# Second dense layer of batches 1 to 3 by one level of Strassen's method

## The chip, the cores and the metric

The kernel runs on one core of one Trainium2 chip. The metric is the device time of one execution in microseconds (us), given as the median of several executions. "Span" is the time from the first to the last instruction of the one profiled execution. It is about 2 us shorter than the time. Ratios are those of one kernel's fast runs to the other kernel's fast runs in the same rounds on the same chip. They are not quite the ratio of the medians quoted beside them.

## The reference

Four batches of attention with a window of 128 keys and 4 sink keys, then two dense layers with a squared ReLU between them:

```python
keep = is_sink | in_window                       # 8 heads, 768 tokens, head_dim 64
a = softmax(where(keep, q @ k.T / 8, -1e9)); attn = a @ v
x = attn.transpose(0, 2, 1, 3).reshape(3072, 512)
r = maximum(x @ w_in, 0)                         # w_in 512 x 2048
out = (r * r) @ w_out                            # w_out 2048 x 512
```

The change works on the last line. The result is compared with a tolerance, so sums of bf16 operands may be rounded in another order.

## The kernel before

Every piece of work is an `Op` with a key, a cost per engine, the ops it comes after and the buffers that it takes. The kernel's own plan puts the ops in order, by earliest start and then by key, and the instructions are issued in that order. The waits in the finished program are derived from what the instructions read and write.

The second dense layer treats a pair of token tiles at a time. Its accumulator is one tile in PSUM of 2 x 512 fp32 a partition. Each 512 of them are called a bank in this text. It is filled by 32 matmuls of 512 columns (only the last pair of all has two tiles, left out here):

```python
def layer2(b, u, keys, by_part=False):
    ...
    for n, (i, part) in enumerate(order):
        def mm(e, i=i, t=t, part=part, n=n):
            if n == 0:
                bank_t["y", b, u] = bank(bs, "py", [128, 2, DM], FP32)
            ...
            for fb in range(4 * part, 4 * part + 4):
                nc.tensor.matmul(pm[:, i, :], lhsT=gT_sb[t // 4][:, fb, 128 * (t % 4):128 * (t % 4) + 128],
                                 rhs=w_out_sb[:, fb, :], start=(fb == 0), stop=(fb == NFB - 1))
    ...
    def evac(e):                                 # the only reader of py
        o = bank_t["osb", b, u] = work["osb"].tile([128, 2, DM], FP32, name="osb", tag="osb")
        copy(e, o, bank_t["y", b, u])
```

The softmax here doesn't subtract the row's maximum and nothing guards it: scores larger than these inputs give would overflow.

Of the kernel before, what the change touches and what calls it, by code (L numbers as in the profile page):

```python
# [20 lines left out]
WARM_UNTIL = 34.0  # L21

# [10 lines left out]
class Op:  # L33
    def __init__(self, key, engines, run, after, takes, reads, dma, follow):
        self.key, self.engines, self.run = key, engines, run
        self.after, self.takes, self.reads, self.dma = list(after), list(takes), list(reads), dma
        self.follow, self.yields, self.margin = list(follow), [], 0.0
        self.end = self.issued = self.engine = None


class Plan:
# [8 lines left out]
    def __init__(self, capacity):  # L50
        self.ops, self.capacity = [], dict(capacity)

    def op(self, key, engines, run, after=(), takes=(), reads=(), dma=0.0, follow=()):
        o = Op(key, engines, run, after, takes, reads, dma, follow)
        self.ops.append(o)
        return o

    def run(self):
# [12 lines left out]
        while left:  # L71
            best = None
            for o in ready:
                t = 0.0
                need = {}
                for s in o.takes:
                    if len(s.pools) > 1:
                        s.pool = min(s.pools, key=lambda p: min(free[p], default=1e9))
                    need[s.pool] = need.get(s.pool, 0) + 1
                ok = True  # L80
                for p, n in need.items():
                    if len(free[p]) < n:
                        ok = False
                        break
                    t = max(t, sorted(free[p])[n - 1] + LATENCY)
                if not ok:
                    continue
                if o.dma:
                    past = landed.get(next(iter(o.engines)), ())
                    if len(past) >= 8:  # L90
                        t = max(t, past[-8])
                pick = None
                for e, c in o.engines.items():
                    slack = PE_SLACK if e == "pe" else 0.0
                    start = max([t + slack if t > 0 else 0.0, engine.get(e, 0.0)] +
                                [a.end + LATENCY + slack for a in o.after if a.engine != e or a.dma] +
                                [a.issued for a in o.follow])
                    if pick is None or start + c < pick[1] + pick[2]:
                        pick = (e, start, c)
                cand = (round(pick[1], 2), o.key)  # L100
                if best is None or cand < best[0]:
                    best = (cand, o, pick)
# [31 lines left out]
def kernel(  # L134
# [28 lines left out]
    sizes = dict(att=2, den=2, qr=5, qs=6, expm=8, r=3, osb=2)  # L163
# [9 lines left out]
    mask = consts.tile([128, 2, 4, 128], BF16)  # L173
    mask0 = consts.tile([128, 2, 4, 128], BF16)
    bias = consts.tile([128, 4, 128], BF16)
    bias0 = consts.tile([128, 4, 128], BF16)
# [10 lines left out]
    xT_sb = [consts.tile([128, NS, NKB, 256], BF16, name=f"xT{i}") for i in range(2)]  # L187
    gT_sb = [consts.tile([128, NFB, w], BF16, name=f"gT{i}") for i, w in enumerate((512, 256))]
# [63 lines left out]
    def build_masks(e):  # L252
        for h2 in range(2):
            for i in range(2):
                nc.gpsimd.tensor_copy(out=mask[:, h2, 2 * i:2 * i + 2, :], in_=tri)
                nc.gpsimd.tensor_copy(out=mask0[:, h2, 2 * i:2 * i + 2, :], in_=tri)
            nc.gpsimd.memset(mask0[0:NSINK, h2, 1:3, :], 1.0)
# [10 lines left out]
    c_fill = op(-9, {"dve": 2.5}, fill)  # L268
# [11 lines left out]
    def dma_op(queue, name, run, us, behind=None, takes=(), yields=()):  # L280

        def go(e):
            ds = run(e)
            if behind is not None:
                for d in ds:
                    after_dma(d, loaded[behind])
            loaded[name] = ds[-1]
        o = op(-5, {queue: (0.85 if queue == "pool" else 0.5) + (0.3 if behind else 0.0)}, go, dma=us, takes=takes,
               follow=[chained[queue]] if queue in chained else (),
               after=[ops[behind]] if behind is not None else ())  # L290
        ops[name] = chained[queue] = o
        o.yields += [ops[y] for y in yields]
        o.follow += [ops[y] for y in yields]
        return o

# [106 lines left out]
    def attention(b, key):  # L402
# [16 lines left out]
        def stage(g, f0, f1, side):  # L419

# [83 lines left out]
            if g == 0:  # L504
# [7 lines left out]
                def sink_values(e):  # L512
                    for j in range(NP):
# [9 lines left out]
                                    after=([ops["turn", b, 1, 0]] if b in NATURAL else copies) + prev_sinks)  # L523
            lo = max(256, t0)
# [20 lines left out]
            for s in range(t0 // 256, last // 256):  # L545
                fs = 0.36 + 0.5 * (256 * s - t0) / (last - t0)
                norms = []
                biased = b == 0 and s < BIASED
                for m0 in (0, 2):
# [27 lines left out]
                    for ms in ((m0,), (m0 + 1,)) if b == 0 else ((m0, m0 + 1),):  # L577
                        sc.append(op(
                            at(fm), {"pe": len(ms) * (0.7 if biased else 0.28) + 0.1}, lambda e, f=scores, ms=ms: f(e, ms),
                            takes=[banks[m - m0] for m in ms],  # L580
                            after=[ops["turn", b, ti, t] for ti in (0, 1)
# [5 lines left out]
                    for j, m in enumerate((m0, m0 + 1)):  # L587
# [7 lines left out]
                        def domask(e, s=s, m=m, o=o):  # L595
                            x = ex_t[b, s, m]
                            if e == "dve":
                                mk = (mask if s else mask0).rearrange("p h a c -> p h (a c)")
                                nc.vector.tensor_mul(x[:, :, o:512], x[:, :, o:512], mk[:, :, o:512])  # L599
                            elif s == 0:  # L600
                                mk = mask0.rearrange("p h a c -> p h (a c)")
                                nc.gpsimd.tensor_mul(x[:, :, o:512], x[:, :, o:512], mk[:, :, o:512])
# [4 lines left out]
                        if biased:  # L607
# [4 lines left out]
                                         {"pool": 1.3, "dve": 0.7} if s else {"dve": 0.58, "pool": 1.1},  # L612
                                         domask, after=[ex] if first else [ex, late["masks"]]))

                    bo = Slot(side, 1)

# [35 lines left out]
                    norms.append(op(at(fm + 0.17), {"dve": 0.95}, norm, after=[va] + prev_bridge, reads=[bo]))  # L652

# [30 lines left out]
    def layer1(b, key, fbs, c0, cw, need):  # L684
        n = len(fbs)
# [14 lines left out]
        def relu(e):  # L700
            r = bank_t[tag, "r"] = work["r"].tile([128, n, cw], BF16, name="r", tag="r")
            if e == "act":
                nc.scalar.activation(out=r, in_=bank_t.pop(tag), func=AF.Relu)  # L703
            else:
                nc.vector.tensor_scalar_max(r, bank_t.pop(tag), 0.0)
# [9 lines left out]
    def layer2(b, u, keys, by_part=False):  # L715

        tail = b == B - 1 and u == NS - 1
        bs = Slot("den", 1)
        bt_ = Slot("den", 1)
# [4 lines left out]
        for n, (i, part) in enumerate(order):  # L724
            t = 2 * u + i

            def mm(e, i=i, t=t, part=part, n=n):
                if n == 0:
                    bank_t["y", b, u] = bank(bs, "py", [128, 2, DM], FP32)
                if tail and n == 4:  # L730
                    bank_t["y", b, u, 1] = bank(bt_, "py", [128, 2, DM], FP32)
                pm = bank_t["y", b, u, 1] if tail and n >= 4 else bank_t["y", b, u]
                for fb in range(4 * part, 4 * part + 4):
# [5 lines left out]
                   takes=[bs] if n == 0 else [bt_] if tail and n == 4 else ())  # L739
# [9 lines left out]
        def store(e):  # L749
            nc.sync.dma_start(out=out[128 * g:128 * g + 256, :].rearrange("(i p) m -> p i m", p=128),  # L750
                              in_=bank_t.pop(("osb", b, u)))

        def evac_tail(i):
            def run(e):
                if i == 0:
                    bank_t["osb", b, u] = work["osb"].tile([128, 2, DM], FP32, name="osb", tag="osb")
                o, y = bank_t["osb", b, u], bank_t["y", b, u] if i == 0 else bank_t["y", b, u, 1]
                if i == 0:
                    copy("dve", o[:, 0, :], y[:, 0, :])
                    nc.sync.dma_start(out=out[128 * g:128 * g + 128, :], in_=o[:, 0, :])  # L760
                else:
                    h = work["qr"].tile([128, DM // 2], FP32, name="half", tag="qr")
                    copy("act", h, y[:, 1, 256:512])
                    copy("dve", o[:, 1, 0:256], y[:, 1, 0:256])
                    nc.scalar.dma_start(out=out[128 * g + 128:128 * g + 256, 256:512], in_=h)
                    nc.sync.dma_start(out=out[128 * g + 128:128 * g + 256, 0:256], in_=o[:, 1, 0:256])
            return run

        if tail:
            e0 = op(keys(0, 3), {"dve": 0.7}, evac_tail(0), after=[ops["layer2", b, 2 * u, 3]], takes=[os_], reads=[bs])  # L770
            op(keys(1, 3), {"dve": 0.5}, evac_tail(1), after=[a, e0], reads=[bt_, os_])
        else:
            ev = op(keys(1, 3), {"act": 1.05, "dve": 1.25}, evac, after=[a], takes=[os_], reads=[bs])
            op(keys(1, 3), {"sp": 0.1}, store, after=[ev], reads=[os_], dma=2.0)
# [32 lines left out]
    for b in range(B):  # L807
        if b == 0:
            at = attention(0, lambda f: f - 1.0)
            at(0, 0.0, 1.0, ("den", "att"))  # L810
            late["masks"] = op(0.006, {"pool": 3.0}, build_masks, after=[c_tri, ops["bridge", 0, 1]])
# [23 lines left out]
        for u in range(NS):  # L835
            if b == 0 and u < 2:
                layer2(b, u, lambda i, part, u=u: 0.408 + 0.466 * (4 * part + 2 * u + i) / 24, by_part=True)
            else:
                layer2(b, u, lambda i, part, u=u, b=b: b + 0.5 + 0.5 * (8 * u + 4 * i + part) / 24)
# [36 lines left out]
```

## Time and profile before

| | before |
|---|---|
| time, median of 3 | 225.88 us (225.76 to 226.05) |
| span of the profiled run | 223.8 us |
| TensorE busy | 215.5 us, 96% |
| VectorE busy | 103.7 us, 46% |
| all waits of TensorE, summed | 3.1 us, of which 0.6 after the first 20 us |
| last matmul to end of span | 3.9 us |

TensorE is the bound: busy in every slice and hardly ever waiting. The prediction shows the lines. The waits tell whether the order of the other engines keeps TensorE fed, and the last row is what no saving on TensorE can touch.

### The profile page before, as it was taken

To read this page: it belongs to the slowest core of one execution; us is meant where nothing else is said; L and a number is where in the kernel's file an instruction comes from. 1 tells how busy PE (TensorE), PEld (TensorE's weight loads), DVE (VectorE), ACT (ScalarE), POOL (GpSimd) and SP (SyncE) were. 2 spreads that over 40 slices of the span, in tenths; PEclk is the share of its full clock that TensorE was granted. 3 is DMA by queue.
4 is the path that set the end of the run, shared out by engine and by line. 5 is a ranking of instruction groups with operands and counts; after the bars stand their busy time and mean duration, and the time that the engine had idled before them with its cause. 6 is when DMAs were issued, how large, how long until landed. Compare 5 with 4: busy or idle time off the path is not lost.

```text
span 223.8 us, 4586 instructions
## 1 busy us (share of the span) xinstructions
PE 215.5 (96%) x1932; PEld 138.2 (62%) x1952; DVE 103.7 (46%) x192; ACT 115.9 (52%) x131; POOL 64.8 (29%) x99
## 2 busy tenths in 40 slices
PE   7899999999999999999999999999999999999993
PEld 7549996467865886555454545598464455874441
DVE  6646346476656764466452536657241024430010
ACT  2695566506893577286727188665351165551010
POOL 7991015055999415997100000000000000000000
PEclk9999999999999999999999999999999999999999
DMA  5999968998999999999999464020221320000222
GB/s 144 289 187 208 208 196 109 199 349 240 131 179 139 150 197 150 122 150 199 143 144 124 139 166 48 0 50 0 47 98 25 116 97 0 0 3 0 94 103 86
DMA packets 84309, 28.13 MB, mean 126 GB/s; under 512 B 70336, under 2 KB 80832, under 8 KB 84288
## 3 DMA queue, kind: packets, MB, share of 16 engines
q0 software_dynamic: 52608, 10.49, 61.9%
q1 hardware_dynamic: 31496, 17.20, 34.9%
q8 instruction: 15, 0.25, 0.4%
q10 hardware_dynamic: 184, 0.14, 0.2%
q14 instruction: 6, 0.05, 0.1%
HBM read 27.30 MB, written 6.29 MB: 150 GB/s over the span
## 4 chain that ended last, share of the span: by engine, by line
PE 91%; DMA 3%; SPq 2%; ACT 1%; DVE 1%; issue 1%; DVEq 0%
PE pm L694 38%; PE py L734 37%; PE po L634 6%; PE ps L571 5%; DMA qr<-in_q_dram 3%; PE pt L476 2%; SPq L348 2%; PE px L671 1%; DVE qkT L208 1%; PE ps L564 1%; PE pk L531 0%; ACT r L703 0%; ACT expm L590 0%; ACT qkT L206 0%; PE px L201 0%
## 5 line engine op out<-in xcount | busy, mean ns | idle before, releaser
L734 PE MATMUL py<-w_out_sb,gT 128*128 128x512 bf16 x366 | 86.1, 379 | 1.1 <-issue 0.3
L694 PE MATMUL pm<-xT,w_in_sb 128*128 128x256 bf16 (+1 forms) x576 | 86.7, 308 | 0.4 <-ACT r L703 0.3
L694 PEld LDWEIGHTS <-w_in_sb 128*128 128x128 bf16 x576 | 63.0, 114 | 20.9 <-issue 1.7
L703 ACT ACTIVATE r<-pm 128x1024 bf16<-128x1024 f32 x48 | 49.2, 1025 | 32.7 <-PE pm L694 23.9
L734 PEld LDWEIGHTS <-gT 128*128 128x128 bf16 x384 | 35.4, 98 | 39.2 <-issue 1.7
L710 DVE TENSOR_TENSOR gT<-r 128x1024 bf16<-128x1024 bf16 x48 | 33.1, 690 | 50.3 <-ACT r L703 50.2
L590 ACT ACTIVATE expm<-ps 128x1024 bf16<-128x1024 f32 (+1 forms) x48 | 43.2, 952 | 17.1 <-PE ps L571 17.1
L599 DVE TENSOR_TENSOR expm<-expm,mask 128x1024 bf16<-128x1024 bf16 (+1 forms) x39 | 25.4, 654 | 23.7 <-ACT expm L590 23.2
L206 ACT ACTIVATE osb<-py 128x1024 f32<-128x1024 f32 x9 | 9.2, 1024 | 31.2 <-PE py L734 31.1
L634 PEld LDWEIGHTS <-expm 128*128 128x128 bf16 x352 | 16.5, 97 | 4.1 <-issue 0.6
L634 PE MATMUL po<-v,expm 128*128 128x65 bf16 x352 | 17.5, 193 | 0.0
L646 DVE TENSOR_TENSOR xn_sb<-po,rc 128x512 bf16<-128x512 f32 x24 | 16.6, 691 | 0.8
L571 PE MATMUL ps<-qkT 64*128 64x128 bf16 (+1 forms) x256 | 14.8, 238 | 0.3
L571 PEld LDWEIGHTS <-qkT 64*128 64x128 bf16 x256 | 8.0, 94 | 10.7 <-issue 9.9
L634 PE MATMUL po<-vs,es 128*128 128x65 bf16 x128 | 13.1, 193 | 0.0
L208 DVE COPY osb<-py 128x1024 f32<-128x1024 f32 (+2 forms) x4 | 3.6, 889 | 19.0 <-PE py L734 15.9
L210 POOL CAST qs<-qr 128x512 bf16<-128x512 f32 x6 | 4.2, 714 | 26.2 <-DVE gT L710 14.1
L634 PEld LDWEIGHTS <-es 128*128 128x128 bf16 x128 | 11.7, 97 | 0.0
L390 POOL DMA_DIRECT2D v<-in_v_dram x12 | 10.8, 918 | 3.4 <-DMA qn<-in_q_dram 2.5
L380 POOL DMA_DIRECT2D qn<-in_q_dram x12 | 10.8, 918 | 1.5 <-DMA qn<-in_k_dram 1.2
L361 POOL DMA_DIRECT2D v<-in_v_dram x12 | 10.9, 926 | 0.5 <-DMA qr<-in_k_dram 0.5
L208 DVE CAST qs<-qr 128x512 bf16<-128x512 f32 x16 | 8.1, 513 | 6.2 <-DMA qr<-in_k_dram 3.1
(51 smaller groups left out, 108.1 us busy)
## 6 DMA issues: line engine op xcount, KB each, us to landing
out_dram<-osb SPq DMA_DIRECT2D x11, 512.0 KB, 2.8
v<-in_v_dram POOLq DMA_DIRECT2D x24, 128.0 KB, 6.5
qr<-in_k_dram SPq DMA_DIRECT2D x8, 256.0 KB, 5.2
qr<-in_q_dram SPq DMA_DIRECT2D x8, 256.0 KB, 4.9
w_in_sb<-in_moe_w_in_dram POOLq DMA_DIRECT2D x4, 512.0 KB, 9.8
w_out_sb<-in_moe_w_out_dram POOLq DMA_DIRECT2D x4, 512.0 KB, 10.8
qn<-in_k_dram POOLq DMA_DIRECT2D x12, 128.0 KB, 7.2
qn<-in_q_dram POOLq DMA_DIRECT2D x12, 128.0 KB, 8.8
```

What stands on the lines that cost most here:

```text
L208: nc.vector.tensor_copy(out=dst, in_=src)
L361: return [nc.gpsimd.dma_start(out=v_sb[b % 2][:, t, :, 0:D], in_=v[b, :, 128 * t:128 * t + 128, :].rearrange("h p d -> p h d"))]
L380: return [nc.gpsimd.dma_start(out=qn_t[b, ti][:, t, :].rearrange("p (h d) -> p h d", d=D), in_=(q, k)[ti][b, :, 128 * t:128 * t + 128, :]. ...
L571: nc.tensor.matmul(ps[:, h2, o:o + w], lhsT=qkT_sb[r, m, 1, c, :], rhs=qkT_sb[r, m, 0, qb:qb + w // 128, :], start=(i == 0 and not biased) ...
L590: nc.scalar.activation(out=x[:, :, o:512], in_=bank_t["s", b, s, m][:, :, o:512], func=AF.Exp, scale=scale)
L599: nc.vector.tensor_mul(x[:, :, o:512], x[:, :, o:512], mk[:, :, o:512])
L634: nc.tensor.matmul(pv[:, i, h2, :], lhsT=lhsT, rhs=rhs, start=(n_ == 0), stop=(n_ == len(mms) - 1))
L646: nc.vector.tensor_tensor(out=xn_sb[:, 2 * s:2 * s + 2, 128 * m0:128 * m0 + 256].rearrange("p i (j h d) -> p j i h d", j=2, d=D), in0=pv[: ...
L694: nc.tensor.matmul(pm[:, i, :], lhsT=w_in_sb[:, fb // 4, kb, fb % 4:512:4], rhs=xT[:, c0 // 256:(c0 + cw) // 256, kb, :], start=(kb == 0), ...
L703: nc.scalar.activation(out=r, in_=bank_t.pop(tag), func=AF.Relu)
L710: (nc.vector if e == "dve" else nc.gpsimd).tensor_mul(gT_sb[c0 // 512][:, fbs[0]:fbs[0] + n, c0 % 512:c0 % 512 + cw], r, r)
L734: nc.tensor.matmul(pm[:, i, :], lhsT=gT_sb[t // 4][:, fb, 128 * (t % 4):128 * (t % 4) + 128], rhs=w_out_sb[:, fb, :], start=(fb == 0), sto ...
```

## The change

The intent is to do a pair of tiles as one 2 x 2 block product with seven products in place of eight. Each product is 8 matmuls of 256 columns. A = g is split by token tile and by half of the 2048 features, and W by half of the features and half of the columns. VectorE forms four sums of blocks of g for each pair, and four of blocks of W once. The accumulator has four quarters, c and b in its first bank and d and a in its second. Each is filled by one product. TensorE later adds a second product onto c, d and a, after c and a have been copied out and d has been added to a copy. Finally VectorE sums the parts. In this excerpt the comments are mine and "..." marks what is cut.

```diff
+    def layer2_fast(b, u, key):
...
+        def region(name):
...
+            h, part = {"c": (0, 0), "b": (0, 1), "d": (1, 0), "a": (1, 1)}[name]
+            return bank_t["y", b, u][:, h, part, :]          # [128, 2, 2, 256], one tile
...
+        p5 = product(0, "c", "s1", 1, True, [o1, ops["wt", 1]], [bs], [s1_])
+        p7 = product(1, "d", "s3", 3, True, [o3, ops["wt", 3]])
+        x0 = taken("x", "c", os_, 0, [p5])                   # copy of c
+        p1 = product(2, "a", a11, w(0, 0), False, low, [ys] if tail else [])
+        p6 = product(3, "b", "s2", 2, False, [o2, ops["wt", 2], x0], (), [s2_])
+        u0 = taken("u", "a", us, 2, [p1])                    # copy of a
+        ex = pair_sum("x", "d", 2, [x0, p7 if tail else p1]) # x += d
+        p3 = product(4, "c", "s4", w(1, 1), False, [x0, o4], (), [s4_])
+        p4 = product(5, "d", a22, 4, False, [ex, ops["wt", 4]] + ([] if tail else [u0]))
+        eu = pair_sum("u", "b", 4, [u0, p3])                 # u += b
...
+        p2 = product(6, "a", a12, w(1, 0), False, [u0] + high)
...
             else:
-                layer2(b, u, lambda i, part, u=u, b=b: b + 0.5 + 0.5 * (8 * u + 4 * i + part) / 24)
+                layer2_fast(b, u, lambda n, u=u, b=b: b + 0.5 + 0.5 * (8 * u + 8 * n / 7.0) / 24)
...
+    P.place(PLACES)          # shifts and stretches the keys of each stage of each batch
     P.run()
```

The rest, left out here, is what makes room and fits the layout. Tokens of a pair are interleaved in the stored rows, so the ReLU reads PSUM with a stride. The masks are smaller, and a PSUM buffer never yet used is no longer charged a wait by the plan. In the last pair the quarter a has a tile of its own, and the last copies are of 128 columns each.

The plan knows what each product must wait for within its bank: p6, which writes into the first bank, comes after the copy of c.

## The prediction

> **What bounds the kernel now.** I read the page first: the busy shares, the slices and the chain that ended last.
>
> ```profile
> span 223.8 us, 4586 instructions
> PE 215.5 (96%) x1932; PEld 138.2 (62%) x1952; DVE 103.7 (46%) x192; ACT 115.9 (52%) x131; POOL 64.8 (29%) x99
> ...
> PE   7899999999999999999999999999999999999993
> ...
> PE 91%; DMA 3%; SPq 2%; ACT 1%; DVE 1%; issue 1%; DVEq 0%
> ```
>
> TensorE is busy in every slice but the first and the last, and 91% of the chain that ended last is TensorE. A busy TensorE could still be waiting unseen, so I then read the waits with TensorE as the engine that waits:
>
> ```profile
> PE pt L201 <- POOL ident L239: 1.5, 1, 1.5
> PE pt L476 <- DVE qs L208: 0.5, 1, 0.5
> PE pm L694 <- ACT r L703: 0.3, 1, 0.3
> PE py L734 <- issue: 0.3, 2, 0.2
> ```
>
> After the first 20 us it waits for about a microsecond in all. So the order of the other engines is already good enough, and only less TensorE work, a shorter start or a shorter end can save time. Third, the last stage in order of time, because the ends of matmuls are modelled, and the readers of complete groups are a better clock:
>
> ```profile
> 183.55 1.02 ACT L703 ACTIVATE r<-pm 128x1024 bf16<-128x1024 f32 x1 [0.70 <-PE pm L694]
> ...
> 185.28 1.02 ACT L703 ACTIVATE r<-pm 128x1024 bf16<-128x1024 f32 x1 [0.70 <-PE pm L694]
> ...
> 195.68 1.02 ACT L703 ACTIVATE r<-pm 128x1024 bf16<-128x1024 f32 x1 [0.72 <-DVE gT L710]
> ...
> 197.42 1.02 ACT L703 ACTIVATE r<-pm 128x1024 bf16<-128x1024 f32 x1 [0.72 <-DVE gT L710]
> ...
> 206.08 1.02 ACT L206 ACTIVATE osb<-py 128x1024 f32<-128x1024 f32 x1 [5.88 <-PE py L734]
> 212.98 1.02 ACT L206 ACTIVATE osb<-py 128x1024 f32<-128x1024 f32 x1 [5.88 <-PE py L734]
> ```
>
> The first two lines are 1.73 us apart, one group of 8 matmuls of 512 columns: 216 ns each. The next two are 1.74 us apart, one group of 16 matmuls of 256 columns: 109 ns each. The last two are 6.90 us apart: one pair of token tiles of the second dense layer, 32 matmuls of 512 columns, 215.6 ns each. There are 12 such pairs in the kernel and nine in batches 1 to 3: 9 x 6.90 = 62 us is what the change works on.
>
> Last, the groups by form, for the cost of an operation on VectorE:
>
> ```profile
> L710 DVE TENSOR_TENSOR gT<-r 128x1024 bf16<-128x1024 bf16 x48 | 33.1, 690 | 50.3 <-ACT r L703 50.2
> L206 ACT ACTIVATE qkT<-pt 128x512 bf16<-128x512 bf16 x11 | 6.5, 595 | 5.0 <-PE pt L476 3.9 <-DVE qkT L208 0.7
> L539 ACT ACTIVATE es<-pk 128x512 bf16<-128x512 f32 x2 | 1.2, 592 | 0.0
> L208 DVE COPY osb<-py 128x512 f32<-128x512 f32 x1 | 0.7, 693 | 15.6 <-PE py L734 15.6
> L208 DVE COPY osb<-py 128x256 f32<-128x256 f32 x1 | 0.4, 425 | 3.1 <-ACT half L206 3.1
> ```
>
> A bf16 product of 1024 elements in SBUF takes 690 ns; 256 and 512 fp32 elements out of PSUM take 425 and 693 ns.
>
> **What the Trainium skill says.** "TensorE: Matmul & The Clock Gate", section "Back-to-back issue gap", gives 262 cycles for 256 columns and 518 for 512 at 2.4 GHz, so 109.2 and 215.8 ns: the trace agrees (109 and 215.6). The same section also gives a sustained 131 ns for 512 columns, which this trace contradicts. Halving the width of a matmul therefore costs almost nothing by itself. "VectorE: DVE Perf Modes", section "The perf-mode tier table", says that a two-input operation runs at two elements a cycle for bf16 in SBUF and at one for any PSUM operand; 690 ns for 1024 in bf16 against 693 ns for 512 out of PSUM agrees. "SBUF — State Buffer", section "Who interferes with whom", says that a VectorE instruction with two SBUF inputs contends with a GpSimd one that reads SBUF. GpSimd computes little after 80 us here (two triangle operations and four small products) and otherwise only issues loads, so I expect little from it; the profile before does not measure it.
>
> **The change part by part.**
>
> *Removed from TensorE.* Each pair of tiles goes from 32 matmuls of 512 columns to seven products of 8 matmuls of 256 columns: 56 x 109.1 ns = 6.11 us in place of 6.90. The saving is 0.79 us a pair, and 9 x 0.79 = 7.1 us in all. The weight loads double per column moved, but one takes 98 ns for gT and even 114 ns for the strided w_in in the rows by form, and the 256-column groups of the first layer still run at 109 ns with the latter. They hide.
>
> *Added to VectorE.* For each pair: four operand sums of 1024 bf16 (2.76 us), two pair sums from PSUM and a last-quarter sum of 256 (3 x 0.425 = 1.28), and the middle sum of 512 (0.69): 4.73 us, nine times 42.6 us. The built order puts nine more copies of 256 columns on it (3.8). Four weight sums of 2048 bf16, (1024 + 151) cycles by scaling the 690 ns row, 1.22 each: 4.9 us. Fewer whole evacuations (-2.3, one of three big ones stays), and one relu (+1.2). From 103.7 to about 154 us of some 218: 70%, still below TensorE.
>
> *ScalarE* loses seven whole evacuations of 1.02 us and takes 17 of 256 columns at 0.38: unchanged within a microsecond. The relu now reads PSUM with a stride of two. The transposed copies already read PSUM with a stride and take 595 ns for 512 elements, against 592 for a dense read, so I price this at zero.
>
> *Latency inside one pair.* In the order of the changed program each product is followed by at least two others before its bank half is written again: 1.75 us for a semaphore, a copy of 0.4 us and a sum of 0.43 us. Batch 3 has nothing else to hide the operand sums behind. But its first sums stand behind the squares of the wide groups only, and 48 narrow matmuls (48 x 109 ns = 5.2 us) stand ahead of the first product; relu, square and two sums need about 1.3 + 0.7 + 1.4 = 3.4 us. They are hidden. Later pairs need 4.7 us of VectorE in 6.1 us of products.
>
> *VectorE in batch 1*, the densest stretch. From 84.0 to 128.9 us it is now busy for 23.0 of 44.9 us. Three pairs add 14.2, and the stretch shrinks to about 42.5: 37/42.5 = 87%. Walking the orders of both engines side by side there, with these durations, each sum is ready 0.5 us or more before its product. I allow 0.7 us for small waits over all three batches.
>
> *Start.* The order now puts 32 first-layer matmuls ahead of the second transposition of the first batch's rows, and issues five warm-up matmuls less. Worth 0 to 0.5 us; I take -0.3.
>
> *End.* Before, the last matmul ends near 219.87 and the rest is this:
>
> ```profile
> 219.89 0.38 ACT L206 ACTIVATE half<-py 128x256 f32<-128x256 f32 x1 [5.88 <-PE py L734]
> 220.30 0.35 ACTq L765 DMA_DIRECT2D out_dram<-half  x1
> 220.31 0.42 DVE L208 COPY osb<-py 128x256 f32<-128x256 f32 x1 [3.12 <-ACT half L206]
> 220.76 0.34 SPq L766 DMA_DIRECT2D out_dram<-osb  x1
> ```
>
> The last store is issued 0.87 us after the matmul and the span ends 3.04 us later. Now both copies have 128 columns (0.28 and 0.29 us by scaling), which saves 0.2, but the order of the sync queue puts two more and larger stores, of 128 and 256 KB, behind the small one: two more issues of 0.35 us. I take +0.5.
>
> Sum: -7.1 - 0.3 + 0.5 + 0.7 = -6.2 us. The time is 2.1 us longer than the span before (225.88 against 223.8), and I keep that: **219.7 us**.
>
> **The rivals.**
> 1. *VectorE becomes the bound in batches 1 and 2.* For: 87% by my count, an in-order queue, sums between masks and norms that attention waits for. Against: the order was built with costs near the measured ones, and the same method left only a microsecond of waits before. If one in three pairs lost 1 us, 3 us come back: about 222.5.
> 2. *The waits inside the pair surface* (a product waits for the bank half to be taken out). Against: two products of slack each time. If 0.4 us per pair: +3.6 us, about 223.
> 3. *The pairs are hidden anyway.* If loads set the pace of batch 1, a faster second layer would only wait. The slices show DMA near 90% up to 110 us, but TensorE waits for no transfer after the start. The last loads are issued by 107 us, for attention that runs from 128 us on. I give this little.
> 4. *Everything hidden and the new keys remove the waits that are there:* -7.1 - 1.5 and no longer end, about 217.5.
>
> **Range and chances.** Rivals 1 and 2 in part give 221.6, the good case 217.9; I take 218.0 to 221.8 as the range. The line for faster by over 2% is 221.36. Faster 0.87, within 2% 0.12, slower 0.01.
>
> **What would show it.** Right: the pairs of batch 3 are about 6.1 us apart; VectorE is near 154 us busy; TensorE near 208; waits of TensorE after 20 us below 2.5 us in total, no single one over 0.6; from the last matmul to the end 4.2 to 4.7 us. Wrong: matmuls of 256 columns slower than 110 ns with these operands, operand sums over 0.75 us, a relu over 1.05 us, or TensorE waiting for sums of the second layer or masks behind them, with VectorE near full in batch 1.

## The result, and the profile after

The changed kernel is correct and took **231.87 us** (median of 4, 230.58 to 233.06), against 225.97 for before in the same rounds: a ratio of 1.0259, 95% interval 1.0219 to 1.03. It is slower, 10 us above the upper end of the predicted range. The profiled execution was the slowest of the four (233.06 us).

The page of the changed kernel, the busy times and the engines on the chain that ended last:

```profile
span 231.4 us, 5127 instructions
PE 212.0 (92%) x2163; PEld 158.5 (68%) x2163; DVE 148.1 (64%) x279; ACT 113.7 (49%) x140; POOL 61.0 (26%) x89
...
PE 79%; DVE 7%; DMA 6%; ACT 3%; issue 2%; SPq 1%; DVEq 0%
```

TensorE is busy for 3.5 us less, the span is 7.6 us longer, and no other engine is near full. TensorE's share of the chain fell from 91% to 79%. VectorE (from 1% to 7%) and ScalarE (from 1% to 3%) took part of its place, although they are idle for 36% and 51% of the span, which is what a chain of short waits looks like. (DMA went from 3% to 6%: a load of batch 1 is on the chain now, see the part on why the prediction was wrong.) The waits of TensorE (what it waited for: us in all, how often, the longest) name them:

```profile
PE py L880 <- DVE osb L901: 3.3, 5, 0.9
PE py L880 <- DVE u L901: 2.6, 5, 0.6
...
PE py L880 <- DVE osb L251: 0.5, 1, 0.5
PE py L880 <- DVE u L251: 0.5, 1, 0.5
PE py L880 <- ACT osb L249: 0.5, 1, 0.5
```

L880 is the matmul of the Strassen products, L901 the sum of a quarter out of PSUM, L251 and L249 the copies. So 13 products stood still behind a reader of the accumulator, for 7.4 us. All waits of TensorE sum to 13.7 us, against 3.1 before.

How it happens is best seen in a pair with nothing between its products, the last of batch 2. This is the timeline (start, duration, engine, line; in brackets how long the engine had been idle and what ended it):

```profile
178.46 1.04 PE L880 MATMUL py<-wt,sg 128*128 128x256 bf16 x8
...
179.34 1.04 PE L880 MATMUL py<-wt,gT 128*128 128x256 bf16 x8
180.41 0.38 ACT L249 ACTIVATE osb<-py 128x256 f32<-128x256 f32 x1 [0.72 <-PE py L880]
180.84 1.03 PE L880 MATMUL py<-w_out_sb,gT 128*128 128x256 bf16 x8 [0.47 <-ACT osb L249]
181.71 1.04 PE L880 MATMUL py<-wt,sg 128*128 128x256 bf16 x8
182.79 0.38 ACT L249 ACTIVATE u<-py 128x256 f32<-128x256 f32 x1 [1.99 <-PE py L880]
183.20 0.42 DVE L901 TENSOR_TENSOR osb<-py,osb 128x256 f32<-128x256 f32 x1 [3.41 <-ACT u L249]
183.68 1.03 PE L880 MATMUL py<-w_out_sb,sg 128*128 128x256 bf16 x8 [0.93 <-DVE osb L901]
184.55 1.04 PE L880 MATMUL py<-wt,gT 128*128 128x256 bf16 x8
...
186.10 1.03 PE L880 MATMUL py<-w_out_sb,gT 128*128 128x256 bf16 x8 [0.52 <-DVE u L901]
186.97 1.24 PE L746 MATMUL pm<-xT,w_in_sb 128*128 128x512 bf16 x5
```

The seven PE lines of L880 are p5, p7, p1, p6, p3, p4 and p2. Each lasts 1.04 us by its line, but the next one starts 0.87 us after it where nothing stops it, so the last 0.17 us overlap. The copy of c needs only p5, whose line ends at 179.50, but it starts at 180.41, after p7. And p1 writes a, in the other bank, but it starts only when the copy of c is over. So products and readers alternate instead of overlapping. The pair takes 186.97 - 178.46 = 8.51 us, not 6.11 and not the 6.90 of before. Of the 2.40 us that are lost, 1.92 are in the three brackets (0.47, 0.93, 0.52). The other 0.48, 0.16 per stop, is the end of the product before the stop, which nothing overlaps now and which the bracket does not count. At 0.16 for each of the 13 stops the whole loss is 7.4 + 2.1 = 9.5 us, an estimate from this trace.

The program as built confirms this reading. Followed back to the instruction that raises its semaphore, the copy of c waits for the last matmul of p7, p1 for the copy of c, the sum x += d for the copy of a, which waits for p6, p3 for that sum, the sum u += b for p4, and p2 for that sum. In every one of these pairs of product and reader the two lie in different banks, but in the same tile. (The sum x += d and p3 are such a pair too: d and c.)

The end is longer as well. The timeline of the last instructions (SPq is the sync queue):

```profile
226.25 0.68 DVE L924 TENSOR_TENSOR osb<-py,u 128x512 f32<-128x512 f32 x1
226.25 0.28 ACT L249 ACTIVATE half<-ya 128x128 f32<-128x128 f32 x1 [3.33 <-PE ya L880]
...
226.85 0.28 DVE L251 COPY osb<-ya 128x128 f32<-128x128 f32 x1
227.16 0.33 SPq L943 DMA_DIRECT2D out_dram<-osb  x1
...
228.03 0.42 SPq L955 DMA_DIRECT2D out_dram<-osb  x1
```

The last matmul ends about 226.2, as the copy that it releases starts at 226.25. VectorE is busy with the middle sum (L924) until about 226.9, so its own copy comes late. The small store on the sync queue waits for VectorE, and two larger ones, issued up to 228.45, stand behind it. From the last matmul to the end it is 5.2 us, 1.3 more than before.

### The profile page after: what moved, and what is told of

Same layout as the page of the kernel before. It is cut to its first block, busy times and chain, and to the rows that moved or that the text cites. A ratio compares the mean times of both kernels' runs of the same rounds, so it can differ in the third digit from the quotient of the medians.

```text
span 231.4 us, 5127 instructions
## 1 busy us (share of the span) xinstructions
PE 212.0 (92%) x2163; PEld 158.5 (68%) x2163; DVE 148.1 (64%) x279; ACT 113.7 (49%) x140; POOL 61.0 (26%) x89
## 4 chain that ended last, share of the span: by engine, by line
PE 79%; DVE 7%; DMA 6%; ACT 3%; issue 2%; SPq 1%; DVEq 0%
PE pm L746 37%; PE py L880 24%; PE py L784 6%; DMA qr<-in_q_dram 6%; PE po L683 5%; PE ps L617 4%; SPq L392 1%; DVE osb L901 1%; DVE qs L251 1%; DVE u L901 1%; DVE qkT L251 1%; PE px L722 1%; ACT u L249 1%; ACT qkT L249 1%; DVE osb L251 1%
## 5 line engine op out<-in xcount | busy, mean ns | idle before, releaser
L757 ACT ACTIVATE r<-pm 128x1024 bf16<-128x1024 f32 x47 | 48.2, 1026 | 41.5 <-PE pm L746 37.1
L880 PEld LDWEIGHTS <-gT 128*128 128x128 bf16 x288 | 27.9, 98 | 8.3 <-issue 5.2
L880 PEld LDWEIGHTS <-sg 128*128 128x128 bf16 x216 | 20.6, 98 | 8.3 <-issue 5.8
L784 PE MATMUL py<-w_out_sb,gT 128*128 128x512 bf16 x96 | 23.4, 380 | 0.0
L649 DVE TENSOR_TENSOR expm<-expm,tri 128x1024 bf16<-128x1024 bf16 x27 | 18.1, 687 | 4.4 <-ACT expm L637 4.3
L880 PE MATMUL py<-w_out_sb,gT 128*128 128x256 bf16 x128 | 16.6, 272 | 3.0 <-DVE u L901 2.1
L880 PE MATMUL py<-wt,gT 128*128 128x256 bf16 x144 | 18.7, 272 | 0.6 <-DVE u L901 0.6
L880 PE MATMUL py<-wt,sg 128*128 128x256 bf16 x144 | 18.4, 273 | 0.2
L251 DVE CAST qs<-qr 128x512 bf16<-128x512 f32 x19 | 9.2, 491 | 9.5 <-DMA qr<-in_q_dram 7.7
L249 ACT ACTIVATE osb<-py 128x256 f32<-128x256 f32 (+1 forms) x11 | 5.5, 501 | 17.8 <-PE py L880 12.4
L880 PE MATMUL py<-w_out_sb,sg 128*128 128x256 bf16 x72 | 9.3, 272 | 3.9 <-DVE osb L901 3.3
```

What stands on the lines that cost most here:

```text
L249: nc.scalar.activation(out=dst, in_=src, func=AF.Copy)
L251: nc.vector.tensor_copy(out=dst, in_=src)
L649: nc.vector.tensor_mul(y, y, tri.rearrange("p (o a) c -> p o (a c)", o=1).to_broadcast([128, 4, 256]))
L757: nc.scalar.activation(out=o, in_=h, func=AF.Relu)
L880: nc.tensor.matmul(y, lhsT=x[:, i, :], rhs=w_[:, i, :], start=first and i == 0, stop=i == HB - 1, skip_group_check=not first)
```

## The experiments

Theory A: the loss is the waits between the two banks of one accumulator tile, which the arithmetic does not need and the plan does not know. Rival B: VectorE is too late with its sums, because it has too much to do or does it in the wrong order. Rival C: the shifted keys, or the rest of the change, made the order worse.

### e1_sbuf_readers: the readers inside a pair take other data

A wrong result. The same instructions run on the same engines in the same order, but the copies and the sums inside a pair no longer read the accumulator, so nothing of the pair waits for them.

```diff
-                copy(e, t_[name], region(of))
+                copy(e, t_[name], w_out_sb[:, 0, 0:256])
-   nc.vector.tensor_tensor(out=t_[name], in0=region(of), in1=t_[name], op=ALU.add)
+   nc.vector.tensor_tensor(out=t_[name], in0=w_out_sb[:, 0, 0:256], in1=t_[name], op=ALU.add)
```

> Wrong result on purpose. The changed kernel with one edit: the four operations that read a product out of PSUM in the middle of a pair (two copies, two pair sums) read a slice of the second layer's weights in SBUF in their place. Same count, size and order of operations on every engine, but no product waits for a reader any more until the end of its pair. Theory A (each reader and the next product wait for one another because both banks of the pair count as one tile): the 7.1 us of TensorE waits at the second layer's products after 82 us go to under 1.5 us, a pair of batch 3 with nothing between takes 6.1 to 6.3 us in place of 8.5, and the time falls from 231.9 to 220.5 to 223.5 us. Theory B (VectorE, now loaded to over 80% in batches 1 and 2, is too slow for TensorE): VectorE does as much as before, so the waits only move to other products, and the time stays at 229 us or above. Theory C (the new order starts batch 1 too early, on loads that come late): the time stays above 228 us.

Measured: 220.99 us (220.61 to 221.89), ratio to before 0.9789 (0.9752 to 0.9825). The gain of 10.9 us is largely the waits on the accumulator inside the pairs: none is left in this run's trace, and they were worth about 9.5 us above. The waits from 20 to 82 us, before any such pair, were also less in this trace (1.9 us against 3.1), so not all of it is the edit. VectorE did the same work (147.8 us busy), so rival B falls as the main cause. This run cannot tell the waits between the banks from those that the method needs within a bank.

### e4_two_tiles_b3: two tiles in batch 3

A correct result. In batch 3, where the attention's PSUM buffers are free, c and b lie in one tile and d and a in another, and a in a third one in the last pair. The middle sum, which read both halves at once, is split in two.

```diff
+        split = b == B - 1
+        ys = Slot("att", 1) if tail or split else bs
+            if split and name == "d":
+                return bank_t["yd", b, u][:, 0, 0, :]
+            if split and not tail and name == "a":
+                return bank_t["yd", b, u][:, 0, 1, :]
+            if split:
+                nc.vector.tensor_tensor(out=o[:, 1, :], in0=region("c"), in1=t_["u"], op=ALU.add)
+                nc.vector.tensor_tensor(out=o[:, 2, :], in0=region("d"), in1=t_["u"], op=ALU.add)
+                return
```

> Correct result. In batch 3 alone, where attention no longer uses its PSUM tiles, the two banks of a pair are two tiles: sums c and b in one, d and a in the other (a in a third in the last pair); the middle sum becomes two of 256 columns. Theory A: of the 4.5 us of TensorE waits after 173 us about 0.5 us of batch 2's pair there stay and up to 1.9 in its first waits, batch 3's go to under 0.7 us, its pairs run at 6.1 to 6.3 us, and the time is 3 to 5 us less, 227 to 229. Theories B and C: no more than 1 us less, since nothing is taken from VectorE and the start is as it was.

Measured: 228.09 us (227.01 to 228.61), ratio 1.0081 (1.0036 to 1.0127), 3.8 us less than the changed kernel although VectorE has more to do. The chain of work of this run from the last pair of batch 2 on (start, duration, what) shows both states side by side:

```profile
177.57 1.76 PE py L888 x16
...
179.79 1.92 PE py L888 x16
...
185.05 1.03 PE py L888 x8
186.08 15.60 PE pm L746 x96
201.68 0.87 PE py L888 x8
202.55 0.87 PE yd L888 x8
```

The batch-2 pair, still in one tile, starts at 177.57 and ends at 186.08, 8.51 us as in the changed kernel. Each stop shows as a gap between two pieces and 0.17 us on a piece of 16 matmuls (1.92 where 16 x 109 ns is 1.75). The products of batch 3 (L888 into `py` and `yd`; the first two are shown) follow each other without a gap.

### e3_no_keys: Strassen's method without the shifted keys

```diff
-    P.place(PLACES)
+    P.place({})
```

> Correct result. The changed kernel with the table of shifted keys emptied: Strassen in batches 1 to 3, the order from the old keys. Theory C (the shifted keys cost time, in batch 1 above all): 229 us or less. If the keys are needed to interleave the pairs with attention (theories A and B have no say): 233 to 237 us.

Measured: 240.11 us (239.07 to 240.63), ratio 1.0624 (1.058 to 1.0667). The keys are no part of the loss. Without them it is 8 us worse, even more than the 233 to 237 us that I expected for that case, so that half of rival C falls.

### e2_rest_alone: neither Strassen nor keys

```diff
-            elif b == 0:
+            else:
                 layer2(b, u, lambda i, part, u=u, b=b: b + 0.5 + 0.5 * (8 * u + 4 * i + part) / 24)
-            else:
-                layer2_fast(...)
-        if b == 0:
-            weight_sums(...)
-    P.place(PLACES)
+    P.place({})
```

> Correct result. Neither Strassen nor shifted keys: what else the change brought (masks read from a small triangle by broadcast and, for the first block, on VectorE alone; output rows paired for one store; the old kernel's special tail taken out; buffers counted as free from the start without a latency). If these are neutral but for the tail: 226 to 228 us. If the change of the rule for free buffers upsets the order: 230 to 234 us.

Measured: 229.17 us (228.63 to 230.74), ratio 1.0156 (1.0109 to 1.0204). That is between the two expectations, so I was wrong to expect it neutral. The waits of TensorE in this run begin with

```profile
PE ps L617 <- ACT expm L637: 1.7, 2, 1.4
```

where before has 0.3 us, in all, for an exponential. The plain layer has no split last copy any more either: from the last copy's start to the end is 4.5 us, against 3.9 before. So the masks, layouts and slots that came along seem to cost something as long as no keys are fitted to them. With the keys and the method on, that cost is not visible as such, and how much of it is left is not settled.

### e7_bank_waits: the waits between the banks lifted

A correct result. Arithmetic, order and tiles are those of the changed kernel. For each product and each reader in different banks of one accumulator the dependency is declared unneeded when the program is built. Waits within a bank stay.

```diff
+        made = {0: [], 1: []}
+        def touch(h, inst, pe):
+            for other, was_pe in made[1 - h]:
+                if pe != was_pe:
+                    tc.declare_no_dep(inst.ins, other.ins, reason="the other bank")
+            made[h].append((inst, pe))
+                    touch(bank_of[name], mm, True)       # each matmul of a product
+                    touch(bank_of[of], r, False)         # each copy and sum inside the pair
```

> The changed kernel with its arithmetic and order untouched, but between a product and a reader that lie in different halves (banks) of the two-bank accumulator the wait is declared unneeded; waits within a half stay. Correct result. Theory A (the loss is the waits between the halves of one tile, found in the run whose readers took other data): 220.5 to 222.5 us, ratio to before 0.977 to 0.985, no wait of TensorE for an add inside a pair over 0.3 us, pairs of batch 3 about 6.1 us apart. Rival A2 (the readers of the same half, which that run had freed as well, carry a good part of the loss): 224 to 228 us. Rival D (reading one half while TensorE writes the other slows either of them): pairs 6.4 us or more, 225 or more.

Measured: 222.47 us (221.38 to 222.99), ratio 0.9842 (0.9816 to 0.9868), 9.4 us less than the changed kernel and close to the 9.5 estimated from its trace. Against before this is a gain of 1.6%. The same pair as above in this run's timeline (L887 is the matmul of the products, L912 the sum):

```profile
174.81 1.04 PE L887 MATMUL py<-wt,gT 128*128 128x256 bf16 x8
175.06 0.38 ACT L249 ACTIVATE osb<-py 128x256 f32<-128x256 f32 x1
175.69 1.04 PE L887 MATMUL py<-w_out_sb,gT 128*128 128x256 bf16 x8
...
177.18 0.42 DVE L912 TENSOR_TENSOR osb<-py,osb 128x256 f32<-128x256 f32 x1 [1.90 <-ACT u L249]
177.44 1.04 PE L887 MATMUL py<-w_out_sb,sg 128*128 128x256 bf16 x8
```

and in its chain of work:

```profile
174.10 6.11 PE py L887 x56
```

The copy of c now runs from 175.06 to 175.44, while p7 writes the other bank, and the products start 0.87 us apart without a bracket. The chain has 56 matmuls, the number of a pair, as one piece of 6.11 us. The reads beside writes into the other bank slowed neither side, so rival D of that expectation falls, and one wait of 0.4 us is left in all on L887.

### e10_readers_freed and e11_products_freed: one side at a time

Two correct kernels with only half of the waits lifted: in e10 a reader no longer waits for products in the other bank, in e11 a product no longer waits for readers there.

```diff
 e10:
-                if pe != was_pe:
+                if was_pe and not pe:
 e11:
-                if pe != was_pe:
+                if pe and not was_pe:
```

> The changed kernel with only one side of the waits lifted: a reader no longer waits for products in the other half, but a product still waits for every reader before it in either half. Theory A, worked out from the durations in the trace of the changed kernel (copy 0.39, sum 0.44, product 0.87, about 0.2 us for a semaphore): only the product after the first pair of sums still waits, about 0.4 to 0.6 us in pairs with nothing between, so 222 to 225 us. If the readers' late start is no part of the loss: 229 to 232 us.

> The changed kernel with the other side lifted: a product no longer waits for readers in the other half, but a reader still waits for every product before it in either half. Theory A: again only one wait of about 0.4 us is left in a bare pair (the sum of the second half ends about 1.1 us after the fourth product, the next product in that half could start 0.87 after it), so 222 to 225 us. If the products' wait for readers of the other half is no part of the loss: 229 to 232 us. Equal times of this run and e10_readers_freed say that it takes both sides together to lose the 10 us.

Measured: 222.55 us (222.19 to 222.97) and 222.55 us (221.71 to 223.4), ratios 0.9854 both, intervals 0.9831 to 0.9878 and 0.9824 to 0.9883. That is the time of e7 within the noise. It takes both sides together to lose the 9 us: a product that must wait for a reader loses little here if that reader could start at once. My size for what is left, 0.4 us or more per bare pair, was too large. In e10's timeline p6 of the same pair starts at 175.85 and p3 at 176.94, which is 1.09 us apart instead of 0.87, so 0.22 us is left. In e11 the same 0.22 stands one product later.

### e8_bank_waits_tail, and e12_bank_tail_again: a shorter end

e7 with the last quarter copied by ScalarE alone and stored on ScalarE's queue, so that the larger stores need not stand behind it.

```diff
-            h = work["qr"].tile([128, 128], FP32, name="half", tag="qr")
-            copy("act", h, y[:, 128:256])
-            copy("dve", o[:, 0, 0:128], y[:, 0:128])
-            nc.scalar.dma_start(out=rows(0, 128, 256), in_=h)
-            nc.sync.dma_start(out=rows(0, 0, 128), in_=o[:, 0, 0:128])
+            h = work["qr"].tile([128, 256], FP32, name="half", tag="qr")
+            copy("act", h, y)
+            nc.scalar.dma_start(out=rows(0, 0, 256), in_=h)
...
-                after=[p2, em], reads=[ys, os_] if tail else [bs])
+                after=[p2] if tail else [p2, em], reads=[ys, os_] if tail else [bs])
```

The last two lines take the copy out of its place behind the middle sum (em).

> As e7_bank_waits, and the end changed: the last quarter is one copy of 256 columns on ScalarE and its store is issued by ScalarE, so that VectorE and SyncE have only the larger rest, which need not wait behind it. If the end of the changed kernel is long because two larger stores stand behind the small one on SyncE: 0.7 to 1.3 us less than e7_bank_waits, last matmul to end of span 3.6 to 4.2 us instead of 4.85. If the end is set by the last product's own store: no difference (0.3 us).

Measured: 221.54 us (220.71 to 222.95), ratio 0.9809 (0.9776 to 0.9842). That is 0.9 us below e7, though the intervals overlap. The traces agree on it: from the last matmul to the end of the span it is 4.2 us, against 4.9 in e7 (last matmul at 215.92, span 220.8). The same program was run once more as a yardstick for the next one:

> The program of e8_bank_waits_tail once more, as the yardstick of e13_no_reader_waits on the same chip: 220.8 to 222.2 us, ratio to before 0.978 to 0.984.

Measured: 220.94 us (220.27 to 222.82), ratio 0.9768 (0.9743 to 0.9792): 2.3% faster than before, and the fastest correct kernel. In e8 the same program was 1.9% faster, a verdict of "unclear" at 2%. The two intervals overlap, so the gain is about 2%.

### e13_no_reader_waits: what the needed waits cost

A wrong result: e12 with the readers of e1, so that the waits within a bank are gone too.

> As e12_bank_tail_again, but the copies and pair sums take other data from SBUF, so no product waits for a reader in its own half either (wrong result on purpose). If the waits that Strassen's method really needs (within a half) cost what the first such run suggested against e7_bank_waits: 0.8 to 1.6 us less than e12_bank_tail_again. If that difference was only the loads of batch 1, whose start varies by a microsecond from run to run: less than 0.4 us.

Measured on the same chip as e12: 220.44 us (220.2 to 221.41), ratio 0.9765 (0.974 to 0.979) against e12's 0.9768. The ratios are equal, the medians are 0.5 us apart and the fastest runs 0.07 us (220.20 and 220.27). So the waits that the method needs cost nothing that can be measured, which here means less than a microsecond. The medians of e1 and e7, 1.5 us apart and from different chips, must then differ mostly for another reason, which is not shown. The first loads of batch 1, in programs with the same early part, were issued at 40.3 us in e1's trace and at 42.3 in e7's, so that is a candidate, not more.

## Why the prediction was wrong

The step that failed is "Latency inside one pair". It said that "each product is followed by at least two others before its bank half is written again", and that is true of the built order, if a bank half is read as a quarter of the accumulator: three others come between. By whole banks, the copies of c and of a each have two products of slack (p7 and p1 before p6, and p6 and p3 before p4). From this I took 1.75 us of slack for a copy and a sum. But the waits in the built program are kept per tile, and the accumulator of two banks is one tile. A reader waited for whatever product had last been issued to either bank, and the next product to either bank waited for that reader. The slack was two products by the banks and none by the tile, and a pair with nothing between its products took 8.51 us, not 6.11. The program could be built and its waits followed back before anything ran; I looked at the order only.

- *TensorE's arithmetic: right.* A pair is 6.11 us wherever nothing stops it (e7), a saving of 0.79 us. TensorE was busy for 212.0 us, where I had said near 208, and for 210.0 in e7.
- *Rival 2, waits inside the pair: right in kind, too small.* I gave it 0.4 us per pair. Lifting the waits between the banks is worth 231.87 - 222.47 = 9.4 us, so 1.04 us per pair on average and 2.40 in a pair with nothing between its products. That is more than the whole saving of 7.1.
- *VectorE's cost: right.* 148.1 us busy for "about 154". The sums of two bf16 blocks took 683 to 689 ns, those of 256 elements out of PSUM 423 and 424, the weight sums 1208 and 1220, and the strided ReLU 1026 against 1025 before. One reading of mine was careless: the row of 693 ns that I set beside the skill's rate for two inputs is a copy, with one input. The sum that fits is the middle one, of 512 elements out of PSUM, and it took 687 ns, so the rate holds. (ScalarE fell from 115.9 to 113.7 us, a little more than "within a microsecond".)
- *VectorE in batch 1 and rival 1: not seen.* From 84 to 129 us it was busy for 33.2 of 45 us, 74% and not 87%, in a stretch that the waits had made longer. In e7, without those waits, it was 35.1 us, 78%. So my sign of being wrong came half true: TensorE did wait for sums of the second layer, but not because VectorE was near full.
- *Rivals 3 and 4: no.* The pairs were not hidden: e7 changes nothing but waits inside them and gains 9.4 us. And the new keys did not remove waits, as the next point shows. (By their own terms rivals 1, 2 and 4 come to 222.7, 223.3 and 217.3 us; I had rounded them to 222.5, 223 and 217.5.)
- *Start, -0.3: not seen.* In the changed kernel's trace the waits of the first 20 us were 3.2 us, against 2.5 before. From 20 to 82 us, where both kernels' second layer is the old one, they were 3.1 against 0.5. e13, with the same order there, has only 1.3 in all after 20 us, so much of this moves from run to run. More on these waits stands below the list.
- *End, +0.5: the right place, too small.* It grew by 1.3 us, and 0.7 of that came back in e8.

The waits from 20 to 82 us have a trace on the chain of the changed kernel that ended last:

```profile
48.12 7.07 DMA qr<-in_q_dram
```

The chain passes through this load of batch 1. Such a load, issued at 47.6 to 48.8 us, is also on the chain in e4, e7, e8, e10, e11 and e12. In before, e1 and e13 no load after 30 us is. So in these traces the waits go with loads that land late. Why they do so in some runs and not in others is open.

On the way from before to after, 5.9 us, the terms are -7.1 from the products, by arithmetic, and +9.4 from the waits between the banks, measured by e7. The remaining +3.6 are not split by an experiment. They are of the size of the longer end (1.3, of which 0.3 went away in e7 and so is in the 9.4 already) and the early waits (0.7 and 2.6 more, in the trace of the slowest of four runs). Of the Trainium skill, the page "PSUM — Partial Sum Buffer", section "PSUM bank collisions raise a hardware error", says to guard PSUM by bank and quadrant, not by address. e7 agrees that a bank is enough: its results were right with TensorE in one bank and a reader in the other.

## What to carry to other kernels

When an accumulator is read in the middle of its life, count the slack by the unit in which the built program waits, not by the unit that the arithmetic needs: follow each wait back to its instruction before believing an order. Give parts that are written and read in turns a tile each, or lift the waits between them where that is safe, as it was between the two banks here. Freeing either the readers or the writers was already enough here. An engine that is 64% busy can still hold up the one that sets the pace, through a chain of half-microsecond stops that no busy share shows.

## What the Trainium skill lacked or had wrong

- "PSUM — Partial Sum Buffer": it gives the bank and quadrant as the unit to guard by, and the bank as the simple version. It lacks that a built program may keep its waits for a whole tile of two banks, which here cost 9.4 us in nine pairs.
- No page that I read for this gives the cost of one whole stop of TensorE behind a reader of PSUM, from product to product. Here it is 0.63, 1.10 and 0.68 us for a copy, a copy with a sum, and a sum (from start to start of the products above, less 0.87).
- "TensorE: Matmul & The Clock Gate", section "Back-to-back issue gap": its sustained 131 ns for 512 columns does not hold here (215.6 ns in the pairs of before); its isolated figures do.
